# The low part of the queries in a tile of 128 rows with zeros, in a recurrence and mixture-of-experts kernel

## The chip, the cores and the metric

The program runs on one core of one Trainium2 chip. The metric is the device time of one execution in microseconds; the median of the runs counts. The core has a matrix engine (TensorE, PE in the profile, with its weight loads as a row of their own, PEld), a vector engine (VectorE, DVE), a scalar engine (ScalarE, ACT), a general engine (GpSimd, POOL) and a queue for transfers (SyncE, SP). Each engine takes its instructions strictly in the order in which they stand in the program and waits on semaphores for the others.

## What is computed

The reference first runs a linear recurrence over 768 tokens for 4 sequences and 8 heads of 48 channels, and then hands its output, 384 channels wide, to four attention experts of 64 channels, of which each token uses two:

```python
for t in range(S):                       # S = 768; state: [B, H, 48, 48]
    cur = einsum('bhd,bhe->bhde', u * k_t, v_t)
    y[:, :, t] = einsum('bhd,bhde->bhe', r_t, state + cur)
    state = w_t[:, :, :, None] * state + einsum('bhd,bhe->bhde', k_t, v_t)
...
for e in range(E):                       # E = 4 experts, x: [4, 768, 384]
    q, k, v = x @ wq[e], x @ wk[e], x @ wv[e]
    scores = where(causal, -1e9, scale * (q @ k.T))
    a = exp(scores - scores.max(-1));  a /= a.sum(-1) + 1e-9
    out += gate_e * (a @ v @ wo[e])      # gate_e: softmax over the two largest logits, else 0
```

The change touches one product alone, `q @ k.T`.

## The kernel before

The work comes in eight units: four sequences, each in two halves of 384 tokens (`g` is 0 or 1). `rwkv` computes the recurrence of a unit, chunk by chunk, two heads at a time; `moe` then runs the experts for the queries of that half. While `moe` works on one unit, `rwkv` of the next one runs beside it, so the recurrence is finished some 70 us before the end and the last unit of `moe` stands alone.

Nothing is placed by hand. Every instruction is handed to a planner (class `Plan`) with a due time and a duration from a small table; the planner lays out the four engines and then emits the instructions in the order of its own clock. The group of score products has durations of its own there, `T_SC`, one for each number of keys.

The scores need more than single precision of the fast product, so queries and keys are each held as a high part and a low part, both in the type float32r. For expert `x` the tile `KS[x]` has 128 rows: 64 with the high part of the keys and 64 with their low part (for odd experts the halves are swapped). `QD[x]` also has 128 rows, the high part of the queries in both halves, so one product of 128 rows yields high by high plus high by low (line 588). The low part of the queries is in `QL`, a tile for each pair of experts, 64 rows for either expert; it is multiplied with the 64 rows of `KS` that hold the high part of the keys (line 589). Both add into the same score tile `sp`, and a third, short product adds the causal mask (line 590):

```python
nc.tensor.matmul(spv()[:, h, :], QD[x]()[:, t], ks[:, o], start=True, stop=False)
nc.tensor.matmul(spv()[:, h, :], QL[x // 2]()[hi, t], ks[hi, o], start=False, stop=h < np_ - 1)
```

One call of `scores` takes 128 queries against `n` keys, `n` being 128, 256 or 384 in the first half of a sequence and 512, 640 or 768 in the second. Up to 512 keys there is one pair of these products as wide as `n`; for 640 and 768 there are two pairs, each half as wide. Four sequences, four experts and six widths make 96 groups, 16 of each width, with 128 products of either kind.

After a group, DVE takes the maximum of `sp` (line 594), ACT the exponentials (line 596), PE transposes these (line 609, `tp`), ACT or DVE copies them out (lines 201 and 203), and PE multiplies with the values (line 632, `yp`). Other names that come up below: `pp` and `vp` are the projections of queries, keys and values (lines 500 and 530), `op` the projection of the output (line 696), `xp` the transposes of the recurrence's output (line 454), which wait for the sums `xn` that DVE makes; `suf` is the first scan of the recurrence on DVE (line 345), and `lt` its input. `ust` are constant tiles that POOL clears at the start.

Of the kernel before, what the change touches and what calls it, by code (L numbers as in the profile page):

```python
# [11 lines left out]
F32 = mybir.dt.float32  # L12
# [18 lines left out]
# Time of an instruction by its shape, in ns: what the order of the instructions is planned with.  # L31
# [16 lines left out]
class Slot:  # L48
    """A buffer of a tag; which one, the plan says. It is made when the first instruction that needs it is emitted."""
# [11 lines left out]
# Time from the end of an instruction to the start of one on another engine that waits for it.  # L61
# [5 lines left out]
class Plan:  # L67
    """Orders instructions: each engine takes, of those whose inputs and tiles are there, the one that is
    wanted first. The instructions are then emitted by the time at which they started."""
# [5 lines left out]
    def add(self, kind, engs, fn, r=(), w=(), want=None):  # L75
        """engs: {engine: ns}; fn(engine) emits. r, w: what is read and written, Slots or (Slot, part)."""
        o = dict(engs=engs, fn=fn, want=(self.now if want is None else want) + OFF.get(kind, 0.0), n=len(self.ops),
                 kind=kind, deps=set(), outs=[], slots=[], ready={})
        for k in r:
            if k in self.writer:  # L80
                o["deps"].add(self.writer[k])
        for k in w:
            if k in self.writer:
                o["deps"].add(self.writer[k])
            o["deps"].update(self.readers.get(k, ()))
        for k in r:
            self.readers.setdefault(k, []).append(o["n"])
        for k in w:
            self.writer[k] = o["n"]
            self.readers[k] = []  # L90
        for k in list(r) + list(w):
            s = k[0] if isinstance(k, tuple) else k
            if isinstance(s, Slot) and s not in o["slots"]:
                o["slots"].append(s)
                s.left += 1
        o["deps"].discard(o["n"])
        self.ops.append(o)
        return o

    def order(self, free, slack=60.0, width=40):  # L100
# [7 lines left out]
        bufs = {}       # tag -> for each buffer, by when each engine is through with it; None while held  # L108
# [15 lines left out]
        while len(done) < len(ops):  # L124
            best = None
            for e in engines:
                c, t0 = [], 1e30
                for want, n in cand[e][:width]:
                    o = ops[n]
                    t = max(free[e], after(o["ready"], e))  # L130
                    for s in o["slots"]:
                        if s.idx is None:
                            a = [after(d, e) for d in bufs[s.tag] if d is not None]
                            if not a:
                                t = None
                                break
                            t = max(t, min(a))
                        elif s.bank:        # two engines don't use a bank at once
                            t = max(t, after(s.ends, e, e))
                    if t is not None:  # L140
                        c.append((t, want, n))
                        t0 = min(t0, t)
                        if t <= free[e]:
                            break
                if not c:
                    continue
                want, n, t = min((x[1], x[2], x[0]) for x in c if x[0] <= t0 + slack)
                if best is None or t + ops[n]["engs"][e] * 0.01 < best[0]:
                    best = (t, e, ops[n])
            if best is None:  # L150
                raise RuntimeError("no instruction can go on: " + str(
                    [(o["kind"], o["want"], [s.tag for s in o["slots"] if s.idx is None])
                     for e in engines for o in (ops[n] for _, n in cand[e][:8])]))
            t, e, o = best
            for x in o["engs"]:
                cand[x].remove((o["want"], o["n"]))
            for s in o["slots"]:
                if s.idx is None:
                    b = bufs[s.tag]
                    s.idx = min((i for i in range(len(b)) if b[i] is not None), key=lambda i: after(b[i], e))  # L160
                    b[s.idx] = None
            end = t + o["engs"][e]
            free[e] = end
            o["t"], o["e"], o["end"] = t, e, end
            for s in o["slots"]:
                s.left -= 1
                s.ends[e] = max(s.ends.get(e, 0.0), end)
                if s.left == 0:
                    bufs[s.tag][s.idx] = s.ends
            for k in o["outs"]:  # L170
                x = ops[k]
                x["ready"][e] = max(x["ready"].get(e, 0.0), end)
                need[k] -= 1
                if need[k] == 0:
                    push(x)
            done.append(o)
# [5 lines left out]
def rwkv_moe(ctx: ExitStack, tc: tile.TileContext, wkr, vY, nat, uN,  # L182
# [41 lines left out]
    act = cst.tile([128, 1], F32, name="act")       # loads the table of the exponential  # L224
# [6 lines left out]
    # the scan over chunks, a row for each column of the state: the state that enters, what the chunks  # L231
    # add, a zero that ends the row; and the decays that follow them
# [6 lines left out]
    for i in range(NP):  # L239
        t = cst.tile([128, D, NX], F32, name=f"ust{i}")  # L240
        (nc.gpsimd if i else nc.vector).memset(t, 0.0)
        ust.append(t)
    u_sb = cst.tile([128, DM], F32, name="u_sb")
# [14 lines left out]
    sel = cst.tile([NG, 3 * E, HD], BF16, name="sel")   # picks the two experts of a pair out of the gates  # L258
    tri = cst.tile([128, E, E], F32, name="tri")        # [e, e2]: 1 where e2 < e
# [13 lines left out]
    def weights(n, src, cols):  # L273
        """A matrix split exactly into two float32r parts."""
# [12 lines left out]
    def rwkv(b, g, v0, v1):  # L287
# [10 lines left out]
        for p in range(NP):  # L298
# [45 lines left out]
            # suffix products inside each chunk, scanned from its end; column 0 of a block: the whole chunk  # L344
# [17 lines left out]
            # what a token adds to its own output  # L362
# [53 lines left out]
            for rows, ys, h in ((slice(0, 64), ysA, 0), (slice(64, 112), ysB, 1)):  # L416
# [3 lines left out]
                if g == 0:      # the state that enters the other half  # L420
# [49 lines left out]
    def moe(b, g, v0, v1):  # L470
# [10 lines left out]
        QL = [sb([128, 384], F32R, f"QL{e}", f"QL{n0}{e}") for e in range(2)]  # L481
# [10 lines left out]
        def proj(ep, qk):  # L492
# [10 lines left out]
            for e in range(2):  # L503
                s_ = slice(64 * e, 64 * e + 64)       # where the expert's rows come out
                x_ = slice(64 - 64 * e, 128 - 64 * e)  # the other half
                if qk == 0:
                    qd, ql = QD[2 * ep + e], QL[ep]
                    for r_ in (s_, x_):
# [3 lines left out]
                        ql()[s_], pp()[s_, 0:384], 0.125, qd()[s_].bitcast(F32), op0=ALU.mult, op1=ALU.subtract),  # L512
                        [pp, (qd, True), (qd, False)], [(ql, e)])
# [23 lines left out]
        def gates():  # L537
            """Softmax over the two largest logits, zero elsewhere."""
# [31 lines left out]
        def scores(x, i):  # L570
            """Scores of expert x for one tile of tokens; their exponentials and sums."""
            hi = slice((x % 2) * 64, (x % 2) * 64 + 64)
# [11 lines left out]
            def mm(e):  # L584
                ks = flat(KS[x]())
                for h in range(np_):
                    o = slice(h * w, (h + 1) * w)
                    nc.tensor.matmul(spv()[:, h, :], QD[x]()[:, t], ks[:, o], start=True, stop=False)  # L588
                    nc.tensor.matmul(spv()[:, h, :], QL[x // 2]()[hi, t], ks[hi, o], start=False, stop=h < np_ - 1)  # L589
# [3 lines left out]
                     [(QD[x], True), (QD[x], False), (QL[x // 2], x % 2), "masks"] + kr, [sp])  # L593
# [7 lines left out]
        def transposes(AT, a, x, i):  # L601
            ii = 3 * g + i
            for j0 in range(0, ii + 1, 4):
# [9 lines left out]
                def ev(e, tp=tp, j0=j0, nj=nj):  # L613
                    src = tp()[:, 0:nj * 128].rearrange("p (j t) -> p j t", j=nj)
                    if j0 == 4:        # the last two key tiles share a tile
# [5 lines left out]
        def attend(ep, ATs):  # L621
            """Values weighted by the exponentials, transposed: two experts on the partitions."""
# [20 lines left out]
        def gather():  # L643
            """The gates over the sums, transposed in three exact parts."""
# [17 lines left out]
        def weigh(ep, yp):  # L662
            """The sums of an expert pair by their gates, in two exact parts."""
# [71 lines left out]
    w = bank("sc", "warm")      # keeps the tensor engine's clock up while its inputs are awaited  # L735
# [23 lines left out]
BUFS.update({f"{n}{e}": 1 for n in ("KS", "QD", "QL") for e in range(E)})  # L759
# [11 lines left out]
def _layout(inputs):  # L771
# [3 lines left out]
    def pairs(a):      # [B, H, S, D] -> [B, half, pair, head, chunk, token, D]  # L775
        return a.reshape(B, NP, 2, 2, NH, C, D).transpose(0, 3, 1, 2, 4, 5, 6)

    def heads(t, rows, cols, fill=0):      # [..., head, D, cols] -> partitions 0.. and 64..
# [24 lines left out]
    def ktiles(a):   # [384, n] -> [128, 3, n]  # L803
        return a.reshape(3, 128, -1).transpose(1, 0, 2)

    def cols(a):     # [E, 384, 64] -> [384, E * 64]
# [26 lines left out]
```

## Time and profile before

| | |
|---|---|
| runs | 500.53 us median of 3 (499.93 to 500.97) |
| span of the profiled execution | 500.3 us, 0.2 us under that median |
| PE busy | 450.2 us, 90% |
| PE weight loads | 332.7 us, 66% |
| DVE busy | 425.7 us, 85% |
| ACT busy | 248.0 us, 50% |
| POOL busy | 170.5 us, 34% |
| mean granted TensorE clock | 0.942 |

Busy times are sums over the span. A matmul counts as busy from its start until its last column has left the array, so two that follow each other closely overlap in the records; how fast PE really gets on is seen in the distance from one start to the next. The granted clock is 1.0 at 2.4 GHz and 0.5 at 1.2 GHz.

### The profile page before, as it was taken

The numbers are of one execution on the slowest core, as the hardware profiler recorded it, in microseconds if no ns is written. First come the engines' busy times: TensorE is split into PE (matmuls) and PEld (weight loads), VectorE is DVE, ScalarE is ACT, GpSimd is POOL, SyncE is SP. The second block draws the span as 40 slices with busy tenths as digits, with TensorE's granted clock in tenths as the row PEclk, the third lists the DMA queues.
The fourth block names the chain that finished last, engine by engine and source line by source line (L and its number), as shares of the span: only waits on it lengthen the run. The fifth ranks groups of instructions, "written<-read, shape, count | busy, mean of one in ns | idle before, by whom it ended". The sixth has DMA issues, their size and how long they took to land.

```text
span 500.3 us, 10885 instructions
## 1 busy us (share of the span) xinstructions
PE 450.2 (90%) x4191; PEld 332.7 (66%) x4196; DVE 425.7 (85%) x866; ACT 248.0 (50%) x609; POOL 170.5 (34%) x218
## 2 busy tenths in 40 slices
PE   6867797999898998999988988999997989999985
PEld 3545676667766766767766666776766658886654
DVE  7999999969979899989999889989998876766561
ACT  3232545544445644655553734655552734575552
POOL 4555744412454244722234243722233240000000
PEclk9795899959898999999998999999997999999999
DMA  7544534222523323522331233522342110100101
GB/s 243 192 152 137 162 101 137 67 96 67 164 63 103 100 91 92 163 85 69 120 111 64 85 101 99 162 84 70 100 129 64 37 54 17 48 0 1 48 1 47
DMA packets 18564, 46.64 MB, mean 93 GB/s; under 512 B 2512, under 2 KB 9936, under 8 KB 18512
## 3 DMA queue, kind: packets, MB, share of 16 engines
q1 hardware_dynamic: 18512, 45.94, 29.5%
q8 instruction: 33, 0.54, 0.5%
q14 instruction: 19, 0.16, 0.1%
HBM read 41.21 MB, written 4.72 MB: 92 GB/s over the span
## 4 chain that ended last, share of the span: by engine, by line
PE 54%; DVE 34%; issue 5%; DMA 3%; ACT 2%; POOL 1%; SPq 0%; DVEq 0%; ACTq 0%; POOLq 0%
PE sp L589 8%; PE pp L500 7%; PE tp L609 6%; PE sp L588 6%; DVE ysB L417 5%; PE vp L530 4%; DVE pre L349 4%; DVE suf L345 4%; PE yp L632 3%; DVE ysA L417 3%; PE op L696 3%; PE sp L590 3%; PE aps L393 2%; DVE mx L594 2%; PE ups L409 2%
## 5 line engine op out<-in xcount | busy, mean ns | idle before, releaser
L596 ACT ACTIVATE a<-sp,mx 128x512 f32<-128x512 f32 (+5 forms) x96 | 60.8, 634 | 46.8 <-DVE mx L594 40.1
L594 DVE TENSOR_REDUCE mx<-sp 128x1 f32<-128x512 f32 (+5 forms) x96 | 58.8, 619 | 23.4 <-PE sp L590 22.6
L609 PE MATMUL tp<-ident,a 128*128 128x128 f32 x336 | 57.4, 290 | 7.3 <-ACT a L596 4.0
L354 POOL TENSOR_TENSOR kt<-lt,suf 128x384 f32<-128x384 f32 x31 | 33.7, 1087 | 81.8 <-PE aps L394 56.6
L201 ACT COPY ATa<-tp 128x512 f32<-128x512 f32 (+3 forms) x73 | 34.6, 477 | 42.7 <-PE tp L609 42.3
L589 PE MATMUL sp<-KS,QL 64*128 64x384 f32 (+4 forms) x128 | 54.7, 427 | 0.0
L588 PE MATMUL sp<-KS,QD 128*128 128x384 f32 (+4 forms) x128 | 51.4, 402 | 0.8 <-ACT a L596 0.5
L609 PEld LDWEIGHTS tp<-ident,a 128*128 128x128 f32 x336 | 39.2, 146 | 13.7 <-ACT a L596 5.4
L433 PE MATMUL yps<-ysA,pre 128*64 128x48 f32 x384 | 39.6, 276 | 7.9 <-issue 4.6
L500 PE MATMUL pp<-xh,wh_qk 128*128 128x384 f32 x96 | 40.8, 425 | 3.8 <-DVE QL L511 3.8
L374 POOL TENSOR_TENSOR xn<-nat,rk 128x144 f32<-128x144 f32 x42 | 29.9, 720 | 38.8 <-DVE rk L370 38.6
L434 PE MATMUL yps<-ysB,mB 112*64 112x48 f32 x384 | 37.9, 275 | 4.1 <-DVE ysB L417 4.1
L589 PEld LDWEIGHTS sp<-KS,QL 64*128 64x128 f32 x128 | 23.9, 187 | 23.1 <-issue 20.1
L364 POOL TENSOR_TENSOR nat<-nat,u_sb 128x288 f32<-128x288 f32 x30 | 26.6, 886 | 36.5 <-DMA nat<-in_nat_dram 20.7
L433 PEld LDWEIGHTS yps<-ysA,pre 128*64 128x64 f32 x384 | 29.5, 154 | 14.1 <-issue 8.4
L358 POOL TENSOR_TENSOR pre<-lt,pre 64x384 f32<-64x384 f32 x25 | 28.5, 1140 | 26.9 <-DVE pre L349 14.0
L409 PE MATMUL ups<-nat,kts 64*64 64x48 f32 x384 | 33.9, 229 | 2.5 <-DVE mB L397 1.2
L632 PE MATMUL yp<-ATa,v_sb 128*64 128x384 f32 (+2 forms) x224 | 35.9, 449 | 0.1
L345 DVE TENSOR_TENSOR_SCAN suf<-lt,one_suf 128x390 f32<-128x390 f32 x32 | 34.6, 1080 | 1.7 <-DMA lt<-in_wkr_dram 1.3
L509 ACT ACTIVATE QD<-pp 64x384 fp32r<-64x384 f32 x64 | 31.0, 484 | 9.1 <-PE pp L500 7.6
L409 PEld LDWEIGHTS ups<-nat,kts 64*64 64x64 f32 x384 | 26.8, 139 | 13.0 <-issue 6.2
L417 DVE TENSOR_TENSOR_SCAN ysB<-ust,wdec 48x384 f32<-48x384 f32 x32 | 34.6, 1082 | 1.0
(137 smaller groups left out, 1200.0 us busy)
## 6 DMA issues: line engine op xcount, KB each, us to landing
lt<-in_wkr_dram SPq DMA_DIRECT2D x31, 579.5 KB, 3.8
nat<-in_nat_dram SPq DMA_DIRECT2D x32, 432.0 KB, 3.3
out_dram<-ob SPq DMA_DIRECT2D x24, 192.0 KB, 1.9
ysB<-in_vY_dram SPq DMA_DIRECT2D x32, 96.0 KB, 2.5
ysA<-in_vY_dram SPq DMA_DIRECT2D x32, 96.0 KB, 2.6
w_qk<-in_wqk_dram SPq DMA_DIRECT2D x1, 768.0 KB, 4.5
w_vg<-in_wvg_dram SPq DMA_DIRECT2D x1, 390.0 KB, 4.5
lt<-in_wkr_dram SPq DMA_DIRECT2D x1, 384.0 KB, 3.2
```

What stands on the lines that cost most here:

```text
L345: plan.add("suf", {"DVE": t_dve(WB)}, lambda e, suf=suf, w_=w_: nc.vector.tensor_tensor_scan(rev(suf()), rev(w_()), rev(one_suf), 0.0, op0 ...
L409: nc.tensor.matmul(ups()[0:64, o], kts()[q, i, 0:64], vn()[q, i, 0:D], start=True, stop=True)
L417: plan.add("ys", {"DVE": t_dve(D * NX)}, lambda e, rows=rows, ys=ys, us=us, wd=wd: nc.vector.tensor_tensor_scan(flat(ys()[rows]), flat(us[ ...
L433: nc.tensor.matmul(yps()[q, o:o + D], pre()[:, c, 0:C], ysA()[:, :, c], start=True, stop=True)
L434: nc.tensor.matmul(yps()[q, o + D:o + 2 * D], mB()[0:112, c, :], ysB()[0:112, :, c], start=True, stop=True)
L500: nc.tensor.matmul(pp()[:, 0:384], w[:, qk, k, cs], x()[:, k, :], start=(k == j == 0), stop=(k == j == 2))
L588: nc.tensor.matmul(spv()[:, h, :], QD[x]()[:, t], ks[:, o], start=True, stop=False)
L589: nc.tensor.matmul(spv()[:, h, :], QL[x // 2]()[hi, t], ks[hi, o], start=False, stop=h < np_ - 1)
L594: plan.add("max", {"DVE": t_dve(n)}, lambda e: nc.vector.tensor_reduce(mx(), spv(), axis=AX.XY, op=ALU.max, negate=True), [sp], [mx])
L596: plan.add("exp", {"ACT": t_exp(n)}, lambda e: nc.scalar.activation(a()[:, 0:n].rearrange("p (a n) -> p a n", a=np_), spv(), AF.Exp, bias= ...
L609: nc.tensor.transpose(tp()[:, j * 128:(j + 1) * 128], a()[:, (j0 + j) * 128:(j0 + j + 1) * 128], ident)
L632: nc.tensor.matmul(yp()[e * 64:e * 64 + 64, lo:384], v_sb[ep]()[:, j, e * 64:e * 64 + 64], at, start=(j == 0), stop=(j == nj - 1))
```

## The change

For each of the four experts a constant tile `qlo[e]` of 128 rows and 384 columns is made. At the start POOL clears those 64 of its rows that lie opposite the low part of the keys. The low part of the queries, which used to be written to `QL`, is written by the same DVE instruction to the other 64 rows of `qlo`. The second product of a score tile then takes all 128 rows of `qlo` and of `KS`; the zeros meet the keys' low part, so the sums are the same. The tiles `QL` are gone. The rest of the diff removes comments.

```diff
+    qlo = []
+    for e in range(E):
+        t = cst.tile([128, 384], F32R, name=f"qlo{e}")
+        nc.gpsimd.memset(t[64 - 64 * (e % 2):128 - 64 * (e % 2)].bitcast(F32), 0.0)
+        qlo.append(t)
...
-        QL = [sb([128, 384], F32R, f"QL{e}", f"QL{n0}{e}") for e in range(2)]
...
-                    qd, ql = QD[2 * ep + e], QL[ep]
+                    qd, ql, qk_ = QD[2 * ep + e], qlo[2 * ep + e], ("qlo", 2 * ep + e)
...
                     plan.add("ql", {"DVE": t_dve(384)}, lambda e_, s_=s_, qd=qd, ql=ql: nc.vector.scalar_tensor_tensor(
-                        ql()[s_], pp()[s_, 0:384], 0.125, qd()[s_].bitcast(F32), op0=ALU.mult, op1=ALU.subtract),
-                        [pp, (qd, True), (qd, False)], [(ql, e)])
+                        ql[s_], pp()[s_, 0:384], 0.125, qd()[s_].bitcast(F32), op0=ALU.mult, op1=ALU.subtract),
+                        [pp, (qd, True), (qd, False)], [qk_])
...
-            hi = slice((x % 2) * 64, (x % 2) * 64 + 64)
...
-                    nc.tensor.matmul(spv()[:, h, :], QL[x // 2]()[hi, t], ks[hi, o], start=False, stop=h < np_ - 1)
+                    nc.tensor.matmul(spv()[:, h, :], qlo[x][:, t], ks[:, o], start=False, stop=h < np_ - 1)
...
-                     [(QD[x], True), (QD[x], False), (QL[x // 2], x % 2), "masks"] + kr, [sp])
+                     [(QD[x], True), (QD[x], False), ("qlo", x), "masks"] + kr, [sp])
```

The durations that the planner uses are untouched, and so is its order. On PE, DVE, ACT and SP the instructions stand one by one as before, with the same waits; only names and line numbers differ. On PE, a group of 640 keys with what stands after it, before:

```order
L588 MATMUL sp_5698<-KS_5098,QD_5525 128x320
L589 MATMUL sp_5698<-KS_5098,QL_5550 128x320
L588 MATMUL sp_5698<-KS_5098,QD_5525 128x320
L589 MATMUL sp_5698<-KS_5098,QL_5550 128x320
L590 LDWEIGHTS identb
L590 MATMUL sp_5698<-causal,identb 128x128
L500 MATMUL pp_5718<-xh_5438,wh_qk 128x384
```

The same place on PE in the changed program:

```order
L593 MATMUL sp_5691<-KS_5093,QD_5519 128x320
L594 MATMUL sp_5691<-KS_5093,qlo_94 128x320
L593 MATMUL sp_5691<-KS_5093,QD_5519 128x320
L594 MATMUL sp_5691<-KS_5093,qlo_94 128x320
L595 LDWEIGHTS identb
L595 MATMUL sp_5691<-causal,identb 128x128
L506 MATMUL pp_5711<-xh_5433,wh_qk 128x384
```

The low part comes from `qlo` in place of `QL`; nothing has moved. On POOL, at the start of the program, where the constant tiles are made, before:

```order
L241 MEMSET ust_88 128x384
L241 MEMSET ust_90 128x384
L241 MEMSET ust_92 128x384
L251 IOTA drow 128x1
L254 IOTA dcol 128x36
L260 IOTA tri 128x16
L358 TENSOR_TENSOR mB_150<-lt_115,pre_144 64x384
```

The same place on POOL in the changed program:

```order
L241 MEMSET ust_92 128x384
L247 MEMSET qlo_94 64x384
L247 MEMSET qlo_96 64x384
L247 MEMSET qlo_98 64x384
L247 MEMSET qlo_100 64x384
L257 IOTA drow 128x1
L260 IOTA dcol 128x36
L266 IOTA tri 128x16
L364 TENSOR_TENSOR mB_158<-lt_123,pre_152 64x384
```

Four clearings now stand ahead of three small index tiles, which DVE reads when it makes its masks at the start.

## Rows read from the trace of the kernel before

**Rows 1.** Busy time by stage: stretch, length, engines, granted clock, transfers.

```profile
42.00:116.00 74.00, 63.45 (x638) 48.27 (x638) 67.00 (x131) 34.01 (x91) 32.91 (x44) 0.83 0.36 113
116.00:229.00 113.00, 105.56 (x1021) 79.79 (x1023) 104.01 (x214) 59.33 (x147) 47.59 (x55) 0.95 0.33 101
229.00:342.30 113.30, 105.24 (x1040) 79.02 (x1040) 103.61 (x213) 59.95 (x150) 42.27 (x52) 0.98 0.32 99
342.30:428.00 85.70, 80.05 (x772) 59.56 (x772) 73.05 (x154) 43.04 (x107) 24.38 (x34) 0.96 0.22 69
428.00:500.30 72.30, 65.21 (x404) 47.02 (x402) 39.44 (x95) 38.32 (x92) 0.36 (x2) 1.00 0.06 23
```

**Rows 2.** The chain of work that ended last, by line, on the page.

```profile
PE sp L589 8%; PE pp L500 7%; PE tp L609 6%; PE sp L588 6%; DVE ysB L417 5%; PE vp L530 4%; DVE pre L349 4%; DVE suf L345 4%; PE yp L632 3%; DVE ysA L417 3%; PE op L696 3%; PE sp L590 3%; PE aps L393 2%; DVE mx L594 2%; PE ups L409 2%
```

**Rows 3.** Timeline, 768 keys: start and duration (us), engine, instruction, idle before.

```profile
464.17 0.42 PE L588 MATMUL sp<-KS,QD 128*128 128x384 f32 x1
464.52 0.18 PEld L589 LDWEIGHTS sp<-KS,QL 64*128 64x128 f32 x1 [0.19 <-issue]
464.52 0.44 PE L589 MATMUL sp<-KS,QL 64*128 64x384 f32 x1
464.89 0.44 PE L588 MATMUL sp<-KS,QD 128*128 128x384 f32 x1
...
465.26 0.43 PE L589 MATMUL sp<-KS,QL 64*128 64x384 f32 x1
...
465.63 0.23 PE L590 MATMUL sp<-causal,identb 128*128 128x128 bf16 x1
```

**Rows 4.** Timeline just after it: products of 128 rows that follow each other.

```profile
465.67 0.42 PE L696 MATMUL op<-wh_o,yh 128*128 128x384 f32 x1
465.75 0.19 PEld L696 LDWEIGHTS op<-wl_o,yh 128*128 128x128 f32 x1
...
465.93 0.34 PE L696 MATMUL op<-wl_o,yh 128*128 128x384 f32 x1
466.10 0.34 PE L696 MATMUL op<-wh_o,yl 128*128 128x384 f32 x1
```

**Rows 5.** Timeline: the narrowest scores, and narrow products of 128 rows.

```profile
65.37 0.33 PE L589 MATMUL sp<-KS,QL 64*128 64x128 f32 x1
65.63 0.23 PE L590 MATMUL sp<-causal,identb 128*128 128x128 bf16 x1
...
407.95 0.28 PE L530 MATMUL vp<-wl_vg,xh 128*128 128x260 f32 x1
408.07 0.28 PE L530 MATMUL vp<-wh_vg,xl 128*128 128x260 f32 x1
```

**Rows 6.** Two stages, line 589 alone: PE and PEld busy, and counts.

```profile
229.00:342.30 113.30, 13.32 (x32) 5.85 (x32) 0.98 0.32 99
...
428.00:500.30 72.30, 11.03 (x26) 4.75 (x26) 1.00 0.06 23
```

**Rows 7.** Busy time in a stretch in which DVE is hardly ever idle.

```profile
76.00:98.00 22.00, 18.14 (x205) 13.77 (x203) 21.64 (x40) 11.68 (x31) 10.89 (x18) 1.00 0.36 114
```

**Rows 8.** DVE's waits for finished scores: whole span, then 428 to 500.3.

```profile
DVE mx L594 <- PE sp L590: 22.6, 35, 3.7
...
DVE mx L594 <- PE sp L590: 9.8, 12, 3.7
```

**Rows 9.** Timeline of the start: POOL's clearings, DVE's second scan.

```profile
2.06 1.13 POOL L241 MEMSET ust<- 128x384 f32 x3
...
9.38 0.97 DVE L345 TENSOR_TENSOR_SCAN suf<-lt,one_suf 128x390 f32<-128x390 f32 x1 [1.35 <-DMA lt<-in_wkr_dram]
```

**Rows 10.** Two stretches at a fall of the clock; three projections within the second.

```profile
374.50:378.40 3.90, 2.02 (x20) 1.43 (x16) 3.85 (x5) 0.96 (x2) 2.85 (x4) 1.00 0.21 57
378.40:385.20 6.80, 6.11 (x22) 5.50 (x22) 6.07 (x13) 1.90 (x4) 2.18 (x3) 0.50 0.30 105
...
384.15 0.96 PE pp L500 x3
```

More of the change, by code (lines that the diff above doesn't have):

```diff
@@ L758 @@
             sc=2, mo=2, rw=2)
-BUFS.update({f"{n}{e}": 1 for n in ("KS", "QD", "QL") for e in range(E)})
+BUFS.update({f"{n}{e}": 1 for n in ("KS", "QD") for e in range(E)})
 BANK = {'s1': 'sc'}
```

## The prediction

> **What bounds the kernel now.** I read the busy times by stage first. From 42 to 428 us the recurrence of the next unit runs beside the experts, and two engines are full at once: in the stage from 229.0 to 342.3 PE is busy for 105.24 of 113.30 us and DVE for 103.61 [rows 1]. After 428 only the experts are left, DVE is busy for 39.44 of 72.30 us, and PE sets the pace. Second comes the chain of work that ended last: lines 589 and 588, the two products of a score tile, hold 8% and 6% of the span, some 70 us, more than any other step [rows 2]. So PE's time in them counts, as long as DVE doesn't stop the gain.
>
> Third, the timeline of one score group, where starts matter and not durations. A product of 384 columns of queries by keys starts at 464.17, the next at 464.52, 464.89 and 465.26, the mask at 465.63: 0.35 to 0.37 us from each to the next [rows 3]. Right behind it stand products of the same width and type that all take 128 rows: the first step is 0.26 (465.67 to 465.93), the second 0.17 (465.93 to 466.10) [rows 4]. The weight loads show why. In the score group the load of QL starts at 464.52, after 0.19 us in which the load path was idle and waited for nothing that the profile shows, and its product starts in the same moment [rows 3]. In the row behind, the load begins at 465.75, 0.08 us after the start of the product that is still running [rows 4]. Where a product of 64 rows meets one of 128, in either direction, PE lets the array run empty first; where all take 128 rows it doesn't.
>
> **The change part by part.** *Both products take 128 rows.* Each of the 128 products with the low part is followed by a step of 0.37 that should become 0.17: 0.20 saved [rows 3, 4]. That holds for 112 of them. In the 16 groups with 128 keys the step is 0.26 (65.37 to 65.63); products of 260 columns with 128 rows follow each other at 0.12 (407.95 to 408.07), and 128 columns should need no more: 0.14 saved [rows 5]. Together 112 x 0.20 + 16 x 0.14 = 24.6 us. The product with the high part has a step out too. In the 32 pairs that come second in a group of two it goes from 0.37 to 0.17: 32 x 0.20 = 6.4. As the first of a group it goes from 0.35 to the 0.26 that the first step has among products of 128 rows, 0.09, in 80 groups: 7.2; for the 16 narrow ones I take nothing. In sum PE gets 24.6 + 6.4 + 7.2 = 38.2 us back, 0.30 for each product with the low part. More columns don't pass, and as the two products of rows 3 step alike with 128 and with 64 rows, I give the larger number of rows no price.
>
> The Trainium skill has a rule against this. What rows 4 show is a weight load under a running product that uses the same 128 rows. "TensorE: Matmul & The Clock Gate", Part 3, The mechanism, says that a weight load overlaps with products in flight only where the row groups differ, and that products on different row groups run side by side. By that rule padding takes the freedom away that the halves had, and the sum would be zero; by the row it is 38.2. The row decides here: no product of 64 rows in rows 3 overlaps its neighbour anyway.
>
> *What of it reaches the end.* The stage from 229.0 holds 32 products with the low part, the last one 26 [rows 6]; the other 70 I spread over the remaining three stages by their length, 19, 29 and 22. At 0.30 each, PE gets 5.7, 8.6, 9.5, 6.6 and 7.8 us back in the five stages. DVE's work there stays as it is, instruction by instruction, so its busy time is a floor. How closely can it be packed? Over 22 us from 76 to 98 it is busy for 21.64, 98% [rows 7]; over a whole stage I take 97%. Then the stages can shrink to 67.00/0.97 = 69.1, 104.01/0.97 = 107.2, 103.61/0.97 = 106.8 and 73.05/0.97 = 75.3 us, by 4.9, 5.8, 6.5 and 10.4 us [rows 1]. I take the smaller of PE's gain and this, a little less where the two are close or where PE's whole gain would have to come through: 4.5, 5.8, 6.5 and 6.0. In the last stage DVE is no limit; of 7.8 I take 7.0, the rest goes into the waits of the last experts. Sum: 29.8 us. What is late next is DVE, in the four stages with the recurrence.
>
> *Four clearings on POOL.* Three of twice the rows take 1.13 us, 0.38 each [rows 9]; four of 64 rows cost between nothing and 1.5 us. DVE's masks wait for the index tiles behind them, but DVE then stands idle for 1.35 us until a transfer lands, at 9.38 [rows 9]. That wait hides them: I take 0, at most 1.5 if it were gone. A tile per expert in place of one per pair adds no wait and moves nothing on PE, DVE, ACT or SP; there is one answer, nothing.
>
> The profiled execution spans 500.3 us, 0.2 under the median. 500.3 - 29.8 + 0.2 = 470.7 us.
>
> **The rivals.** *A: DVE's queue keeps most of its pace.* DVE waits 22.6 us in all for finished scores, 9.8 of it in the last stage, so 12.8 before [rows 8]. If only those waits can go and other work of DVE's doesn't move up, 12.8 + 7.0 = 19.8 us are gained (481); if another wait takes half of them, 13.4 (487). For it: both engines are near 92% in the steady stages, so each waits for the other in many small places. Against it: a queue whose inputs all come sooner starts all of its work sooner.
>
> *B: PE sets the whole time.* Nothing of the 38.2 us is lost: 462; the stage from 42 to 116, which runs at a granted clock of 0.83 [rows 1], could also come out faster if denser work were granted more, down to some 457. For it: lines 588 and 589 hold 70 us of the chain. Against it: DVE would have to be busy for over 98% of whole stages.
>
> *C: slower, by the clock.* If PE is through sooner, it waits longer for DVE. In the stretch from 374.5 to 378.4 PE is busy for 2.02 of 3.90 us, waiting for the recurrence's sums; in the 6.8 us behind it the granted clock is 0.50, which is 1.2 GHz, and three projections take 0.96 us, 0.32 each, against 0.17 at 2.4 GHz [rows 4, 10]. A microsecond at the low level thus loses about 0.46 of PE's. In the four stages, 386 us, the granted clocks of 0.83, 0.95, 0.98 and 0.96 amount to 48 us at the low level [rows 1]. The gain of 29.8 is eaten up from 65 us more, which is a mean clock of about 0.85 over the four stages where 0.94 is granted now. Were all as low as the first stage, 0.83, it would be 131 us, 83 more: 38 lost, 8 more than gained, 509 us. Against it: the same waits come back in each unit, and from 229.0 to 342.3 they cost the clock only 0.02.
>
> *D: the change doesn't do what it says.* The step could belong to a product that adds into the tile of the one before, or to the load itself, whatever its rows: 500 to 502. Against it: the products of rows 4 also add into one tile, and load as much.
>
> **How the numbers follow.** The forecast, 464 to 477, has a chance of 0.55; A, 477 to 488, 0.25; B, 455 to 464, 0.12; C 0.05; D 0.03. What this kernel's runs can tell from no change is about 0.2%, 1 us. Only C is slower by more, part of it and part of D are within: faster 0.93, the same 0.03, slower 0.04. The range reaches from 457, B's lower end, to 484, in the middle of A: C, D, half of A and the tip of B stay outside, some 2 in 10.
>
> **What would show it.** Within a score group of 384 columns the starts should lie 0.17 apart and 0.26 to 0.28 for the first, the load of the low part should start under the product before it, and lines 588 and 589 should fall behind the projections in the chain. DVE's share should rise to about 97% from 116 to 342, and its waits for finished scores should shrink to a few us. The last stage should be about 65 us long. Steps of 0.35 would make D right; right steps with DVE still near 92% would make A right; more low-clock stretches than now, C. I am wrong above all if DVE's small waits, for ACT, POOL and transfers, grow as those for PE go.

## The result and the profile after

The changed kernel takes 483.65 us (483.08 to 486.86) where the kernel before took 500.23 beside it: a ratio of 0.968, 95% interval 0.964 to 0.972. It is 16.6 us faster where 29.8 were forecast. A repeat on another chip gave 483.98 us, 0.966 (0.961 to 0.971). Ratios, here and below, leave out executions in a second, slower state (two of four in e4, one of four in e6 and e8), while the times are medians over all of them. What became faster on PE did so as forecast, and by the forecast amount; what that is worth at the end was put too high.

First the timeline of a score group of 768 keys in the changed kernel, PE and its weight loads: start, duration, instruction. It answers [rows 3].

```profile
446.50 0.42 PE L593 MATMUL sp<-KS,QD 128*128 128x384 f32 x1
446.58 0.19 PEld L594 LDWEIGHTS sp<-KS,qlo 128*128 128x128 f32 x1
446.76 0.34 PE L594 MATMUL sp<-KS,qlo 128*128 128x384 f32 x1
...
446.94 0.34 PE L593 MATMUL sp<-KS,QD 128*128 128x384 f32 x1
...
447.11 0.34 PE L594 MATMUL sp<-KS,qlo 128*128 128x384 f32 x1
...
447.29 0.23 PE L595 MATMUL sp<-causal,identb 128*128 128x128 bf16 x1
```

The steps from start to start are 0.26, 0.18, 0.17 and 0.18 us, where they were 0.35 to 0.37. The load of the low part begins at 446.58, while the product of 446.50 runs.

Then the chain of work that ended last, by line, which answers [rows 2]:

```profile
DVE mx L599 4%; PE tp L614 4%; PE pp L506 3%; PE yp L637 3%; DVE ysB L423 3%; PE vp L536 3%; PE sp L593 3%; DVE suf L351 3%; DVE pre L355 2%; DVE ysA L423 2%; PE op L701 2%; PE sp L594 2%; PE ups L415 1%; DVE KS L524 1%; DVE rk L376 1%
```

The score products (lines 594 and 593), 8% and 6% before, hold 2% and 3%, and DVE's maximum stands first, though by a hair: 4%, as much as PE's transposes.

The stages are cut at the same DVE instructions as those of [rows 1], to 0.2 us. The columns are the stretch, its length, the busy time of PE, PEld, DVE, ACT and POOL, the granted clock, and transfers:

```profile
44.00:113.80 69.80, 54.80 (x641) 43.69 (x641) 66.50 (x130) 33.90 (x91) 35.12 (x44) 0.93 0.38 118
113.80:225.50 111.70, 100.68 (x1009) 79.94 (x1011) 104.08 (x213) 58.42 (x146) 46.78 (x55) 0.92 0.33 102
225.50:336.10 110.60, 99.11 (x1051) 78.80 (x1048) 103.60 (x214) 60.50 (x152) 43.69 (x52) 0.97 0.33 101
336.10:416.40 80.30, 72.40 (x776) 57.50 (x775) 72.88 (x155) 43.10 (x108) 25.51 (x34) 0.98 0.24 73
416.40:482.40 66.00, 57.47 (x402) 45.42 (x400) 39.19 (x95) 38.12 (x91) 0.36 (x2) 0.99 0.07 25
```

Against [rows 1] the five stages are 4.2, 1.3, 2.7, 5.4 and 6.3 us shorter; forecast were 4.5, 5.8, 6.5, 6.0 and 7.0. The stretch ahead of them is some 2 us longer, 44.0 against 42.0. From trace to trace that makes 17.9 us. DVE's busy times are the same as before to 0.5 us in every stage. PE is idle for 45.4 us in the first four stages, where it was idle for 31.7.

The trace of the repeat shows how far two executions of one kernel lie apart: cut in the same way, its stages start at 43.3 us, the four take 375.1 us where these take 372.4, and the last one 66.1. Differences of under some 3 us in the four stages say nothing by themselves.

Who waits for whom in the changed kernel (engine and line, what it waits for: us in total, times, longest), first DVE's longest waits over the whole span, then PE's:

```profile
DVE mx L599 <- PE sp L595: 8.0, 12, 3.4
DVE yr L684 <- PE gb L674: 3.7, 4, 2.6
DVE gT L665 <- PE yp L637: 3.2, 1, 3.2
DVE ATa L203 <- PE tp L614: 3.0, 6, 0.8
...
PE xp L460 <- DVE xn L447: 8.1, 5, 3.5
PE tp L614 <- ACT a L601: 6.5, 7, 1.5
```

DVE's wait for finished scores fell from 22.6 [rows 8] to 8.0 us, of which 3.5 lie in the four stages, where it was 12.8. What is left is spread over many places, and PE waits more for DVE and ACT.

### The profile page after: what moved, and what is told of

It is laid out like the page before. It is cut to its first block, busy times and chain, and to the rows that moved or that the text cites. A ratio compares the mean times of both kernels' runs of the same rounds, so it can differ in the third digit from the quotient of the medians.

```text
span 482.4 us, 10894 instructions
## 1 busy us (share of the span) xinstructions
PE 417.1 (86%) x4196; PEld 324.9 (67%) x4196; DVE 424.6 (88%) x866; ACT 247.5 (51%) x609; POOL 177.1 (37%) x222
## 4 chain that ended last, share of the span: by engine, by line
DVE 28%; PE 27%; issue 3%; POOL 3%; ACT 2%; DMA 0%; POOLq 0%; ACTq 0%; DVEq 0%
DVE mx L599 4%; PE tp L614 4%; PE pp L506 3%; PE yp L637 3%; DVE ysB L423 3%; PE vp L536 3%; PE sp L593 3%; DVE suf L351 3%; DVE pre L355 2%; DVE ysA L423 2%; PE op L701 2%; PE sp L594 2%; PE ups L415 1%; DVE KS L524 1%; DVE rk L376 1%
## 5 line engine op out<-in xcount | busy, mean ns | idle before, releaser
L614 PE MATMUL tp<-ident,a 128*128 128x128 f32 x336 | 59.3, 296 | 14.0 <-ACT a L601 6.5
L360 POOL TENSOR_TENSOR kt<-lt,suf 128x384 f32<-128x384 f32 x31 | 34.9, 1125 | 69.5 <-PE aps L400 48.3
L593 PE MATMUL sp<-KS,QD 128*128 128x384 f32 (+4 forms) x128 | 48.7, 382 | 3.6 <-ACT a L601 1.5
L594 PE MATMUL sp<-KS,qlo 128*128 128x384 f32 (+4 forms) x128 | 42.4, 333 | 0.0
L370 POOL TENSOR_TENSOR nat<-nat,u_sb 128x288 f32<-128x288 f32 x30 | 28.0, 934 | 37.7 <-DMA nat<-in_nat_dram 22.8
L439 PEld LDWEIGHTS yps<-ysA,pre 128*64 128x64 f32 x384 | 29.8, 149 | 15.7 <-issue 7.3
L415 PE MATMUL ups<-nat,kts 64*64 64x48 f32 x384 | 35.2, 236 | 4.5 <-DVE mB L403 2.1
L415 PEld LDWEIGHTS ups<-nat,kts 64*64 64x64 f32 x384 | 27.9, 146 | 15.6 <-issue 6.2
L358 ACT COPY wdec<-suf 128x288 f32<-128x288 f32 x32 | 22.6, 708 | 29.5 <-DVE ysB L423 15.3
L423 DVE TENSOR_TENSOR_SCAN ysB<-ust,wdec 48x384 f32<-48x384 f32 x32 | 36.7, 1145 | 1.0
L423 DVE TENSOR_TENSOR_SCAN ysA<-ust,wdec 64x384 f32<-64x384 f32 x32 | 32.1, 1002 | 3.1 <-ACT ust L201 2.8
```

What stands on the lines that cost most here:

```text
L360: plan.add("kt", prod(384), lambda e, k_=k_, sfv=sfv, kt=kt: E_[e].tensor_tensor(kt(), k_(), sfv()[:, :, 1:C + 1], op=ALU.mult), [(lt, 1), ...
L415: nc.tensor.matmul(ups()[0:64, o], kts()[q, i, 0:64], vn()[q, i, 0:D], start=True, stop=True)
L423: plan.add("ys", {"DVE": t_dve(D * NX)}, lambda e, rows=rows, ys=ys, us=us, wd=wd: nc.vector.tensor_tensor_scan(flat(ys()[rows]), flat(us[ ...
L439: nc.tensor.matmul(yps()[q, o:o + D], pre()[:, c, 0:C], ysA()[:, :, c], start=True, stop=True)
L594: nc.tensor.matmul(spv()[:, h, :], qlo[x][:, t], ks[:, o], start=False, stop=h < np_ - 1)
L614: nc.tensor.transpose(tp()[:, j * 128:(j + 1) * 128], a()[:, (j0 + j) * 128:(j0 + j + 1) * 128], ident)
```

## Experiments

Two theories. **Theory 1:** from 42 to 428 us DVE's queue sets the pace, in an order in which DVE, PE and ACT take turns; PE's gain mostly becomes PE's waiting there, and only the last unit hands it on. **Theory 2:** PE still sets the pace, and something on PE itself, the clock above all, took the rest of the gain. The runs e2, e3 and e5 have the order of the changed kernel, e4 and e6 that of the kernel before.

**e1: the clearings behind the index tiles.**

```diff
+    for e in range(E):
+        nc.gpsimd.memset(qlo[e][64 - 64 * (e % 2):128 - 64 * (e % 2)].bitcast(F32), 0.0)
```

> The changed kernel with its four clearings on POOL moved behind the three index tiles, so that DVE's masks no longer wait for them. In the changed kernel DVE stands 1.4 us behind the kernel before at 16 us and 1.8 us behind at 42 us. Theory 1 (the clearings delay the first unit and the delay is carried along): 481.9 to 482.4 us, 1.3 to 1.8 us under the changed kernel. Theory 2 (the transfer that DVE waits for at 9.4 us hides them, as the prediction had it): the same as the changed kernel within 0.5 us.

Measured: 483.70 us, 0.964 (0.959 to 0.968) of the kernel before. Against 0.966 and 0.968 for the changed kernel that is no difference that the times can tell. The traces can. This is the start of the changed kernel: start, duration, engine, instruction, and in brackets the idle time before and what ended it.

```profile
3.25 1.83 POOL L247 MEMSET qlo<- 64x384 f32 x4
...
5.33 0.24 DVE L272 TENSOR_SCALAR onehot<-dcol,drow 128x36 f32<-128x36 f32 x1 [1.06 <-POOL dcol L260]
...
9.18 2.02 POOL L364 TENSOR_TENSOR mB<-lt,pre 64x384 f32<-64x384 f32 x1 [3.78 <-issue]
...
9.55 0.95 DVE L351 TENSOR_TENSOR_SCAN suf<-lt,one_suf 128x390 f32<-128x390 f32 x1
```

And this with late clearings:

```profile
3.58 2.22 POOL L268 MEMSET qlo<- 64x384 f32 x4
...
3.74 0.41 DVE L273 TENSOR_SCALAR onehot<-dcol,drow 128x36 f32<-128x36 f32 x1
...
7.71 1.26 POOL L365 TENSOR_TENSOR mB<-lt,pre 64x384 f32<-64x384 f32 x1 [1.92 <-DVE pre L356]
```

DVE's wait of 1.06 us is gone, and POOL's first product starts 1.5 us sooner. (Its 2.02 us are not the clearings' doing: in the repeat of the changed kernel it takes 1.21.) At 16 us DVE stands 1.1 us ahead of the changed kernel, but only 0.5 ahead of the repeat. The profiled executions end at 481.4 here, at 482.4 and 484.5 in the two of the changed kernel, which lie further apart than the effect. So theory 1's mechanism is there at the start, at 0.5 to 1.1 us and not 1.3 to 1.8; that it reaches the end is not shown.

**e2: without the product of the low part** (it is left out; the rest stands as it did).

```diff
-                    nc.tensor.matmul(spv()[:, h, :], QD[x]()[:, t], ks[:, o], start=True, stop=False)
-                    nc.tensor.matmul(spv()[:, h, :], qlo[x][:, t], ks[:, o], start=False, stop=h < np_ - 1)
+                    nc.tensor.matmul(spv()[:, h, :], QD[x]()[:, t], ks[:, o], start=True, stop=h < np_ - 1)
```

> The changed kernel without the second product of each score tile (the low part of the queries by the keys is left out, 128 products; everything else stands in the same order). It takes another 22 us of PE's time away, the sum of the steps behind these products in the changed kernel. Theory 1 (from 42 to 428 us DVE's queue sets the pace and only the last unit hands PE's gain on in full): about 4 us from the last unit and 1 to 4 us from the rest, 475 to 479 us. Theory 2 (PE still sets the pace and the rest of the expected gain was lost to the clock or by chance): 16 to 22 us, 462 to 468 us.

Measured: 484.48 us, 0.966 (0.961 to 0.971), the same as the changed kernel. Theory 2's 462 to 468 is out of reach, but theory 1's 475 to 479 was not met either. Its stages, cut at the same DVE instructions, columns as above:

```profile
43.90:113.90 70.00, 58.30 (x625) 46.90 (x625) 66.83 (x130) 33.36 (x91) 34.79 (x44) 0.83 0.36 118
113.90:225.30 111.40, 99.85 (x990) 79.42 (x992) 103.10 (x212) 59.28 (x147) 47.62 (x55) 0.89 0.32 102
225.30:338.40 113.10, 99.51 (x1010) 78.48 (x1008) 103.97 (x213) 59.71 (x150) 41.70 (x52) 0.91 0.32 99
338.40:420.20 81.80, 71.33 (x748) 55.66 (x745) 73.61 (x155) 42.69 (x107) 24.92 (x34) 0.94 0.22 72
420.20:484.50 64.30, 54.07 (x376) 41.93 (x375) 38.50 (x95) 38.02 (x91) 0.36 (x2) 1.00 0.07 25
```

The granted clock is lower in all four stages: 0.83, 0.89, 0.91 and 0.94 where it was 0.93, 0.92, 0.97 and 0.98. A clock of c over a stage is 2(1 - c) of it at 1.2 GHz, so that is 78 us at the low level, against 37 in the changed kernel (45 in its repeat). PE has less to do and does it more slowly; the four stages together take 376.3 us, no less than the 372.4 and 375.1 of the changed kernel, and the last one only 1.7 us less. This run alone thus can't part the theories. One thing its trace does tell. In the four stages DVE is idle for 9.9 us within the stretches at the low level (78.3 us in all) and for 18.9 outside them; in the changed kernel it is 6.3 (in 37.7 us) and 19.0. So where the clock was full, less work on PE left DVE's idle time as it was.

**e5: the first product twice.** It puts PE's work back without the long steps between products of 64 and 128 rows.

```diff
+                    nc.tensor.matmul(spv()[:, h, :], QD[x]()[:, t], ks[:, o], start=True, stop=True)
                     nc.tensor.matmul(spv()[:, h, :], QD[x]()[:, t], ks[:, o], start=True, stop=False)
```

> The changed kernel with the first product of each score tile issued twice: 128 products more, all of 128 rows, whose result the second one overwrites. That puts some 22 us on PE (0.17 us for 384 columns) without any step in which the array runs empty; DVE's work and all orders stay. Theory 1 (PE has slack from 42 to 428 us, DVE's queue sets the pace there): 4 to 5 us more from the last unit, 1 to 6 us from the rest, 5 to 11 us over the changed kernel. Theory 2 (PE's time counts nearly in full everywhere): 18 to 22 us over the changed kernel. Theory 3 (the lower clock, which falls where PE waits, ate the gain): the mean granted clock rises over that of the changed kernel and the time rises by under 4 us.

Measured: 488.12 us, 0.973 (0.969 to 0.977); the changed kernel took 483.98 beside it. 128 more products cost 4.1 us. By the steps from start to start they take 19.6 us of PE's time (69.4 for all score products, where it was 49.8), some 15 of them in the four stages. By stage:

```profile
43.30:113.40 70.10, 58.52 (x657) 47.94 (x658) 67.35 (x131) 34.07 (x91) 32.84 (x44) 0.90 0.37 118
113.40:223.00 109.60, 100.55 (x1031) 81.97 (x1030) 104.39 (x213) 58.41 (x145) 47.81 (x55) 0.96 0.33 104
223.00:334.80 111.80, 102.41 (x1077) 82.49 (x1077) 103.66 (x213) 59.99 (x151) 42.93 (x52) 0.97 0.32 100
334.80:417.40 82.60, 75.45 (x812) 60.98 (x810) 72.45 (x154) 43.62 (x109) 24.91 (x34) 0.99 0.24 71
417.40:486.70 69.30, 61.54 (x429) 49.55 (x427) 39.27 (x95) 38.22 (x91) 0.36 (x2) 1.00 0.07 24
```

In the last stage 3.3 us come on top; the four stages ahead of it take 374.1 us, between the 372.4 and the 375.1 of the changed kernel. Theory 2 asked for 18 to 22 us; theory 1 for 5 to 11, so even that was a little high. The clock went up slightly: 31 us at the low level in the four stages, 37 and 45 in the changed kernel. So theory 3 is not shut out for a part of it. But 6 to 14 us less at the low level give PE back some 3 to 6 us, at the prediction's 0.46 for each; the other 9 to 12 us of new work disappeared in PE's idle time.

**e3 and e4: DVE's maximum over half of the columns** (the other half is left out), on the changed kernel and on the kernel before.

```diff
-            plan.add("max", {"DVE": t_dve(n)}, lambda e: nc.vector.tensor_reduce(mx(), spv(), axis=AX.XY, op=ALU.max, negate=True),
+            plan.add("max", {"DVE": t_dve(n)}, lambda e: nc.vector.tensor_reduce(mx(), spv()[:, :, 0:w // 2], axis=AX.XY, op=ALU.max, negate=True),
```

> The changed kernel with DVE's maximum taken over the first half of the columns of each score tile only (the other half is left out; same order). DVE gets about 22 us back in 96 instructions (0.52 ns for each of 448 columns on average), some 17 of them before the last unit. Theory 1 (DVE's queue sets the pace): 12 to 20 us faster than the changed kernel, 464 to 472 us. Theory 2 (PE sets the pace): 0 to 6 us, 478 to 484 us.

> The kernel before with the same halved maximum. Theory 1, that DVE set the pace of the four stages already before the change and PE's steps only came on top: 8 to 14 us faster than the kernel before, 486 to 492 us. Theory 2, that PE alone set it before and DVE only after the change: 0 to 5 us faster, 495 to 500 us. If the gain here is far under that of the same edit on the changed kernel, the two engines limit each other, and a gain on one alone can't come through.

Measured: on the changed kernel 471.22 us, 0.940 (0.935 to 0.945), some 13 us less than the changed kernel. DVE's busy time over the span fell by 20.0 us, from 424.6 to 404.6. By stage:

```profile
43.90:111.70 67.80, 53.20 (x641) 42.49 (x641) 65.47 (x130) 33.85 (x91) 35.00 (x44) 0.95 0.38 121
111.70:220.60 108.90, 98.56 (x1012) 78.29 (x1011) 100.15 (x213) 58.75 (x146) 46.60 (x55) 0.94 0.34 104
220.60:326.90 106.30, 97.57 (x1043) 78.53 (x1040) 97.87 (x214) 59.36 (x151) 43.33 (x52) 0.97 0.33 105
326.90:404.10 77.20, 71.89 (x784) 57.71 (x782) 67.67 (x155) 43.08 (x109) 25.24 (x34) 0.97 0.24 76
404.10:469.70 65.60, 57.33 (x404) 45.61 (x402) 34.55 (x95) 37.85 (x91) 0.36 (x2) 0.98 0.07 25
```

In the first four stages DVE's busy time fell by 15.9 and the stages by 12.2, to 360.2 us: three quarters of what DVE saves there reaches the end. The clock doesn't explain it: here too 31 us are at the low level, as in e5, whose four stages take 374.1. On the kernel before 493.72 us, 0.976 (0.967 to 0.984), some 12 us less, though the four runs spread from 486.60 to 498.71. In its trace, of a run of 495.17 us, the four stages are 8.6 us shorter than before. Both gains lie in theory 1's ranges (12 to 20 and 8 to 14), e4's with less certainty: DVE set the pace beside PE already before the change. The sign that e4 was also to look for, a gain far under that of e3, didn't come: in this order of the instructions relief and padding add up, as far as e4's wide interval can tell, 2.4% and 3.3%, and 6.0% together.

**e6: padding (the tile of 128 rows with zeros) in the last unit alone,** `spare[0]` being true there, with late clearings.

```diff
+        pad = spare[0]
...
+                    if pad:
+                        nc.tensor.matmul(spv()[:, h, :], qlo[x][:, t], ks[:, o], start=False, stop=h < np_ - 1)
+                    else:
+                        nc.tensor.matmul(spv()[:, h, :], QL[x // 2]()[hi, t], ks[hi, o], start=False, stop=h < np_ - 1)
```

> The kernel before with the padding in the last unit alone (its four experts; the other seven units keep products of 64 rows), clearings behind the index tiles. Theory 1 (in the last unit PE sets the pace and a gain comes through in full): 6 to 7 us faster than the kernel before, which is over a third of the whole effect for 24 of 128 products. Theory 2 (the gain is worth the same everywhere): 24/128 of 16.6 us, 3 us.

Measured: 493.42 us, 0.983 (0.979 to 0.988), 8 us faster than the kernel before (6 to 11 by the interval). Fewer than a fifth of the products bring about half of the gain; 3 us, as an even worth would have it, lies outside. Its trace, of the longest of the four runs, puts the gain where it should be: its last stage is 67.1 us long, where it was 72.3, and the four stages are no shorter, 388.2 where they took 386.0. (I wrote 24 products; the last unit has 20, four experts with one, two and two.)

**e7 and e9: the copies of PE's results, out of PSUM, its memory for them, on ACT,** except in the last unit, with padding (e7, late clearings) and without (e9). The engines stand in the same order in both.

```diff
     def evac(cols):
+        if not spare[0]:
+            return {"ACT": t_act(cols)}
         return {"ACT": t_act(cols), "DVE": t_dve(cols)}
```

> The changed kernel with late clearings and with all copies out of PSUM given to ACT, except in the last unit; before, the planner put some 30 us of them on DVE. The planner makes a new order. Theory 1 (DVE's queue sets the pace from 42 to 428 us): DVE loses about 25 us there and the kernel gets 8 to 18 us faster than the changed one, 466 to 476 us. Theory 2 (PE or the clock): within 4 us of the changed kernel, or slower, as ACT's longer queue delays PE.

> The kernel before, products of 64 rows, with the copies given to ACT as in e7; all four engines then stand in the order of e7. Against e7 it tells what the padding is worth once DVE has 19 us less to do. Theory 1 (DVE's queue held the padding's gain back): the padding is worth clearly more than the 17 us that it brought beside DVE's full queue, 22 to 32 us, so this kernel takes 488 to 498 us. Theory 2 (part of the 38 us is lost on PE itself or to the clock, whatever DVE does): the padding is worth 13 to 18 us here too, 479 to 484 us.

Measured: with padding 465.80 us, 0.930 (0.925 to 0.934), at the lower end of theory 1; without 491.25 us, 0.981 (0.974 to 0.989). The planner gave DVE other work in return, so DVE lost 19 us (424.6 to 405.6) and not 25. The page's busy times and DVE's longest wait, with padding:

```profile
PE 412.6 (89%) x4196; PEld 321.7 (69%) x4196; DVE 405.6 (87%) x818; ACT 264.6 (57%) x673; POOL 163.9 (35%) x206
...
DVE mx L602 <- PE sp L598: 10.9, 16, 1.4
```

and without:

```profile
PE 452.3 (92%) x4196; PEld 332.3 (67%) x4196; DVE 406.8 (83%) x818; ACT 266.5 (54%) x673; POOL 160.8 (33%) x202
...
DVE mx L596 <- PE sp L592: 31.4, 46, 2.3
```

The four ratios stand side by side: the relief of DVE alone brings 1.9%, padding alone 3.2 to 3.4%, both together 7.0%. As the relief brings a new order with it, what of the 1.9% is DVE's and what the order's is not told apart. Padding is worth 17 us beside DVE's full queue and 25 beside the relieved one (491.25 to 465.80, 1 us of it perhaps from the late clearings). Theory 1 gave 22 to 32, theory 2 13 to 18. In this order padding and relief are worth more together than one by one; in the order of e3 and e4 they were not. Without padding, the relieved DVE only waits longer for finished scores: 31.4 us where it was 22.6 [rows 8].

**e8 and e10: elementwise products of the recurrence on POOL,** alone and with e7's edit.

```diff
-FLEX, LATE, SLACK = (True, True, 60.0)
+FLEX, LATE, SLACK = (False, True, 60.0)
```

> The changed kernel with late clearings and with all elementwise products of the recurrence's later units given to POOL, which the planner shared between POOL and DVE (some 30 us of them on DVE). New order by the planner. Theory 1 (DVE sets the pace): 5 to 15 us faster than the changed kernel, 469 to 479 us. Rival: POOL takes 1.1 us where DVE takes 0.8 and DVE's scans slow down beside it, so the recurrence gets later: same or slower, 484 to 495 us.

> e7 and e8 together: copies on ACT, elementwise products on POOL, low part padded. Theory 1: DVE gets shorter once more and PE comes to set the pace; if e8 gains, this one lies 3 to 8 us under e7, 458 to 463 us. Rival: POOL's slower products delay PE and the result is e7's or worse, 466 to 475 us.

Measured: e8 477.44 us, 0.952 (0.944 to 0.960), some 6 us under the changed kernel, with DVE at 408.3 us; that agrees with theory 1, though its runs went from 472.19 to 480.85 and the planner made a new order here too. e10 466.75 us, 0.935 (0.930 to 0.941): no gain on e7. DVE is down to 388.7 us, but PE has 412.1 of 464.3. That is the rival's time; whether POOL's slower products or a PE that is 89% busy, as in e7, stand behind it wasn't told apart.

**The repeat of the changed kernel,** the mark for e5 to e7.

> The changed kernel once more, as the mark for the runs beside it. All theories: 0.965 to 0.971 of the kernel before.

Measured: 0.966, as given above. The best kernel of all is e7, 0.930 of the kernel before.

## Why the prediction was right in kind and wrong in size

**The steps of PE: right.** The long steps are gone and the new ones have the lengths taken from [rows 4]. Summed over both traces, the time from the start of each score product to the next start fell from 88.4 to 49.8 us, by 38.6; the prediction had 38.2. The weight load under a running product on the same 128 rows is there in the timeline above, so rival D is out. "TensorE: Matmul & The Clock Gate", Part 3, The mechanism, of the Trainium skill says that a weight load overlaps with products in flight only where the row groups differ. The load at 446.58, 0.08 us after the start of a product on the same 128 rows, differs from that, and the measurement decides. "TensorEngine Tiling (Array Packing)", Key Properties, of the Trainium skill says that a change of the tiling mode drains TensorE. That agrees with 0.35 to 0.37 us before and 0.17 to 0.26 after; the traces show the late load and the step, not the empty array itself.

**The last stage: nearly right.** 7.0 forecast; 6.3 in the traces, 5 in the trace of e6 and 8 (6 to 11) by its times.

**DVE's share: wrong, and this is the step that failed.** I let the four stages shrink until DVE would be 97% busy, or nearly, on the strength of 22 us in which it is 98% busy [rows 7]. DVE's floor held: its busy times did not move. But it got to 66.50/69.80 = 95%, 93%, 94% and 91%. The forecast lengths of the four stages come to 363.2 us and leave DVE 15.5 us of idle time; it is idle for 25.3. These 9.8 us are most of what is missing: between the 29.8 us forecast and the 17.9 traced, 9.2 are lost in the four stages, 2.0 ahead of them and 0.7 in the last. Nor did DVE's small waits grow, as I feared. Without the waits for finished scores its idle time in the four stages was 25.5 us and is 21.8: it stayed, where the forecast needed it to shrink to under 15.5. A stretch in which DVE happens to have its inputs at hand tells nothing of a stage in which its work alternates with PE's and ACT's: an in-order queue at 93% can be what sets the pace. That it does so is shown from both sides, at the same 31 us of low clock: some 15 us more on PE cost the four stages nothing that two executions can tell (e5), and 15.9 us fewer on DVE gave 12.2 (e3).

**The kernel was limited by both engines before.** Taking the smaller of two bounds was the right form, but each engine's small waits for the other are a third term. Rival A had that: 481 to 487 (477 to 488, with a chance of 0.25), and the result lies in it, at the very edge of the stated range and outside the forecast of 464 to 477. Its sign, right steps with DVE still near 92%, is what came. Its price, that only the waits for finished scores go, fits in the main: in the four stages they fell from 12.8 to 3.5 us, by 9.3, and the stages shrank by 13.6.

**The four clearings: mis-sized.** I took 0, hidden by DVE's wait for a transfer, with 1.5 as the bound. DVE's second scan starts only 0.17 us later (9.55 for 9.38), as forecast, but POOL's first product starts at 9.18 (7.58 before), and PE waits for it until 11.26 (10.44 in the repeat, 8.85 before); at 16 us DVE is 1.4 us behind, 0.9 in the repeat. I followed the one queue and not the engine behind it. From the first's start to the last's end the four took 1.83 us, over the bound.

**The clock: rival C didn't happen, but it isn't idle.** In the four stages there are 37 us at the low level (45 in the repeat) where there were 48. The falls lie elsewhere than before, so parts of the trace gain or lose by them alone. The stage that fell shortest, from 113.8 to 225.5 with 1.3 us of 5.8, is the only one in which the granted clock went down by more than 0.01, from 0.95 to 0.92:

```profile
184.50:194.80 10.30, 10.30 (x104) 7.98 (x101) 7.21 (x21) 4.19 (x13) 2.05 (x2) 0.50 0.34 102
```

Here PE is never idle, at the low level, and DVE is idle for 3.1 us. How much of that stage's 4.5 us is the clock's is open; in e5, at 0.96, with more work on PE, it is 2.1 us shorter. Over all four stages the clock alone is not what failed: 6.3 of DVE's 25.3 idle us lie at the low level, and the other 19.0 are still more than the 15.5 of the forecast.

## What to carry to other kernels

Where products of 64 and 128 rows alternate on TensorE, count the changes of height: padding the smaller one with zeros cost nothing per product here and took 0.1 to 0.2 us off a step of 384 columns. But turn a gain on one engine into time by asking what the other engine's queue does over a whole stage: two engines at 92% each hold each other, and what a relief of one is worth depends on the other. Relief of both was worth more than the two alone added up with copies on ACT and a new order (7.0% against 1.9% and 3.3%), and just the sum with a shorter maximum in the old order (6.0% against 2.4% and 3.3%, the 2.4 with a wide interval). A best stretch is not a bound that a stage will reach.

## What was not expected of the hardware

With less work on PE the granted clock fell: 0.908 to 0.925 on average in the four runs without the low product (e2), 0.933 to 0.949 in the changed kernel and its repeat, 0.947 to 0.959 with a product more (e5). So a product left out can be paid for, in part at least, by those that stay.

A clearing of 64 rows by POOL isn't cheaper than one of 128. Four take 1.83 us from the first's start to the last's end, 0.46 each, and 2.22 in e1; three of 128 rows take 1.13, 0.38 each [rows 9].
